# Rows grouped by residue by the host; a fused FFT-convolution and MLP block with unmasked tiles and exchanges through DRAM

## The chip, the cores and the metric

The kernel runs on one core of a Trainium2 chip. The metric is the device time of one execution in microseconds (us), lower is better. Engines are named as in the profile: PE (TensorE matmul), PEld (its weight loads), DVE (VectorE), ACT (ScalarE), POOL (GpSimd), SP (SyncE, which issues all DMAs of this kernel). Data is bfloat16, sums are float32 in PSUM, which has eight banks of 128x512 float32.

## The reference

All activations are 2048 tokens by 512 channels, batch 1.

```python
def _A_ref(q, k, v, shift_k, ssm_k, ssm_D):
    k_shift = 0                              # 4-tap causal shift of k along the tokens
    for t in range(4):
        k_shift = k_shift + k_pad[:, t:t + S, :] * shift_k[:, 3 - t]
    kv = k_shift * v
    # causal convolution of kv with ssm_k along the tokens, by FFT of length 4096
    y = irfft(rfft(pad(kv)) * rfft(pad(ssm_k)))[:, :S, :]
    y = y + kv * ssm_D
    return q * y

def _B_ref(x, w1, w2, w3, w4):               # w1, w2: 512x512, w3: 512x1792, w4: 1792x512
    h = gelu(layernorm(x) @ w1)
    # four groups of 128 channels, moved by -1, +1, -2, +2 tokens
    hs = concat([g0, g1, g2, g3]) @ w2
    x1 = x + hs
    return x1 + gelu(layernorm(x1) @ w3) @ w4

h  = A_q + _A_ref(layernorm(A_q), A_k, A_v, A_shift_k, A_ssm_k, A_ssm_D)
h2 = h + _B_ref(layernorm(h), B_w1, B_w2, B_w3, B_w4)
```

## The kernel before

**Halves and rows.** A token has the number 1024*s + 8*p + b: half s (0 or 1), partition p (0 to 127), block b (0 to 7). The two halves are called first (s=0) and second (s=1). The long convolution is done by halves: A0 and A1 are the transforms of the two halves of kv, F0 and F1 those of the filter. The first half of the output needs A0*F0, the second A0*F1 + A1*F0.

**Tasks.** The body describes some 800 tasks (`add(name, engines, function, dependencies, ...)`) and then emits them in an order written out by hand in the string `ORDER`, where each word gives a task, its engine and its PSUM banks or buffers. Each engine works off its own words strictly in that order. The names used below:

- `S1(sig,b,hp)`, step 1 of a transform (L397): 8 matmuls of 128 rows by 32 columns, N=512, with tables `f1` whose entries are masked so that only rows p of the right residue modulo 4 count. There are 8 tasks for each of F0, A0, F1, A1. `E1` copies their result from PSUM (L266; two banks, 128x1024).
- `X(sig,g,kl)` (L412): a DMA within SBUF, from each fourth partition of `z1` (32 of them) to each second one of `z2` (64), 256 KB. 8 for each signal.
- `S2(sig,kl)` (L420): 16 matmuls of 64 rows by 32 columns. `E2` copies their result (L266); for F1 it is instead a "fold" of two DVE operations (L432) that subtract and add the result of F0.
- `P(s,kl,...)` (L481): products of spectra on DVE, 128x1024, 16 for the first half and 32 for the second. `I2` (L493): 32 matmuls of 32 rows by 32 columns, N=512, 8 tasks for the first half and 16 for the second. `EV` copies (L266).
- `XI(s,kl)` (L503): a DMA within SBUF, 512 KB, four for each half. `I1(s,b)` (L511): the last inverse step, 8 matmuls of 64 rows by 128 columns, masked table `f2`.
- `K` (L449) and `KV` (L457): the shift of k as matmuls with diagonal matrices, and the product with v on DVE. `Q`: statistics of q (L516).
- `H` (L619): the row h on DVE. `HS`, `uw`, `rr`, `hn`: its statistics and normalisation factors over ACT, DVE and POOL. `hb`: the normalised row (L655, L653). `LT` and `TE`: its transpose, either on PE (L671) with a copy, or by two DMAs to DRAM (L664) and a transposing DMA back (L666), as the set `BYDMA` says.
- `W` (L700), `U`: w1 and gelu. `X2` (L729), `S` (L732), `SS`, `R` (L736): w2, the sum, its statistics, the residual. `lb`, `LX`, `EX`: second normalisation and transpose.
- `M` (L781), `G` (L785), `O` (L793), `Z` (L795), `OUT` (L797): w3 for two chunks of 128 features over 256 tokens, gelu, w4 over 14 chunks, the last sum, the store. 56 tasks M, 16 tasks O.
- `Lw1` to `Lw4` and the other loads: L275.

```python
    def step1(b, hp, src):
        def f(e, sl):
            for hh in range(2):
                for t in range(2):
                    for b0 in range(2):
                        j = 2 * t + b0
                        nc.tensor.matmul(ps[32 * j:32 * j + 32, sl[hh], :], lhsT=f1t[:, 4 * t + 2 * hp + hh, :],
                                         rhs=src(2 * b + b0), start=True, stop=True)
```

Of the kernel before, what the change touches and what calls it, by code (L numbers as in the profile page):

```python
# [9 lines left out]
P = 128  # L10
# [6 lines left out]
XW = 258  # L17
KW = NB * 129 + 4
# [13 lines left out]
029P7 004S 030P 031V 067P01 069P23 005S 033A 068A 041V 042G 070A 003S 037V 008S 036V 040V 063P45 002S 064A 065P67 066A 059P01 046V 099P30 043V 000S  # L32
060A 047V 001S 007S 006S 034G 038A 032V 044V 035G 105P2 010S 100V 091P71 061P01 039A 055P45 106V 009S 048A 021S 092V 056A 340V 101P6 102V 103P3 104V
045A 062A 097P2 098V 015S 022S 342V 023S 343V 093P7 057P45 019S 053G 119P01 058A 120A 095P6 049G 050V 121P23 051A 094V 054G 017S 122A 115P45 117P01
118A 024S 078S 096V 111P67 113P23 114A 116V 107P45 112V 109P01 110A 108V 074S 088P6723 090V 089A 345V 077S 071S 073S 075S 085P0145 087V 079P6723 127S
086A 130S 128S 123S 081A 344V 219P10 220V 080A 131P2345 133A 132V 124S 134P6701 135V 136A 072S 076S 082P2345 083A 084A 223P1 125S 144V0 129S 137P6723
020S 227P01 138A 143V1 146V2 147V3 139A 145P45670 148P 231P3 224V 149M 150A 228V 346V 152V0 012S 126S 187P01 189P45 188A 190A 153V1 155V2 018S 232V
014S 195P67 011S 183P01 196V 185P23 184A 186V 013S 191P45 192A 151S 025S 156V3 140P6701 142A 141A 154P23451 157P 347V 225P1 016S 197P67 158M 159A 198A
221P0 201S 161V0 162V1 226V 199S 200S 193P23 194A 341V 163P45670 202S 348G 165V2 164V3 166P 168A 167A 222V 160S 233P1 204S 229P0 170V0 171V1 174V2
239P23 173V3 203S 349G 172P45671 234V 240A 175P 230V 177A 176V 350G 354G0 207P0123 052A 208V 206S 209V 235P67 216P4501 217V 236A 351G1 241P67 242A  # L40
271V0 169S 339G 205S 243P23 244A 178S 179P54 218V 237P67 238A 355V 360G0 247P23 336S 352V 357G1 335S 180P10 361V 358V 356A 338S 245P67 248A 353A 375V
249P45 181P03 246A 366G0 367V 250A 182P12 255S 363G1 251S 364V 376G 377V 362A 359A 372G0 365A 252S 213P4567 215V 378A0 369G1 379P30 381A1 373V 374A
026S 027S 382P2 380A 370V 272V1 259P6701 254S 383A 260A 388G 389G 390G 214V 274V2 275V3 258S 386P3 371A 387A 210P4567 212V 211V 256S 261A 273P01230
391A0 392P71 394A1 395P6 276P 277V0 413G 414G 393A 396A 368A 278V1 262P4567 281V2 415G 401G 253S 402G 403G 280V3 263A 028S 279P 257S 282P 283M 284A
416V0 399P5 400A 384P4 385A 418S 417V1 419S 286V0 268P0123 420S0 264V 269A 397P7 398A 287V1 289V2 270V 404G0 290V3 265P4501 266A 288P23671 291P 406S
423P5 405A1 292V0 424A 293V1 296V2 267A 294P 421P4 295V3 297P 422A 285S 298A 407S 513P5 302V0 301V1 303P01230 304V2 408S0 305V3 306P 299A 509P4 514V
307V0 308V1 411P5 515A 409P7 510V 511A 310V2 311V3 309P 312P 412A 317V0 410A 521P7 313A 300S 314A 517P6 316V1 320V2 319V3 318P01451 522V 321P 322V0
525P3 337S 573G 574G 575G 579A0 576A1 323V1 325V2 577P70 578A 529P2 580P7 315S 326V3 523A 324P 581A 518V 519A 602G 603G 604G 605G0 327P 329A 328A
582P70 588P6 594P5 430V 431V 429V 584P4 426V 585A 330S 583A 425V 592P1 593A 586P0 427V 589A 587A 428V 432V 433V 590P4 591A 526V 530V 434G 527V 606A1
331P76 332P43 333P21 531A 435V 439G0 595A 516V 440V 599P5 436A1 441A 437V 445G0 442G1 630V 438V 446V 451A0 443V 608S 596P0 631G 632G 607S 609S0 600V0  # L50
601S 460G 461G 334P37 444A 447A 473G 452V 448A1 633V0 635S 610P60 614P1 634V1 611A 616P5 620P6 449V 612P4 450V 457G0 453V 454A1 618P2 615A 462G 466A0
613A 617A 458V 622P7 636S 637S1 638P10 644P5 623A 455V 463V1 464P70 465A 621A 459V 619A 524V 640P4 456V 467P3 645A 646P7 474G 475V 477G1 479S 468V
469P6 471P5 497V 520V 498G 624P3 476A0 499V 478S 528V 480S0 472A 470A 500A1 625V0 502S 533P6 534V 485G 501A0 503S 504S1 537P5 538V 648P3 650P6 649A
539A 535V 483P5 484A 486G 487V 642P3 643A 489V0 491S 481P2 647A 488G1 627P5 658G 659G 660G 482A 512V 597V1 532V 662A0 507P7 490S 492S0 641A 661A1 663S
508A 505P4 495P0 493P7 506A 541P4 545P3 626S 546V 639A 494A 496A 553P7 557P2 561P3 651A 549P6 547A 554V 542V 543A 742V 743G 562V 563A 598S 555A 558V
744V 745A1 550V 569P4 565P7 566V 664S 665S0 666P30 667A 674P2 675A 678P6 652P7 655P3 560V 746V0 748S 628V0 672P5 564V 629S 747S 749S1 676P2 570V 571V
750P40 751A 668P1 669A 548V 756P0 551V 757A 686G 687G 688V 677A 690V0 692S 752P4 753A 689V1 552V 673A 670P1 671A 559V 760P2 761A 762P5 691S 714V 715G
716V 754P4 718G0 717V1 693S0 758P2 759A 694P10 696P0 653V0 654S 704P7 719S 568V 679A 705A 680P2 700P7 540V 695A 536V 763A 702P6 698P5 755A 767P4 720S
656V1 567V 657S 699A 701A 770G 771G 697A 706P7 721S1 722P50 772G 773G0 730P3 774G1 731A 556V 776S 724P1 725A 544V 775S 683P0 684V0 777S0 734P3 703A
764P6 707A 778P70 784P1 685S 728P0 785A 735A 765V0 766S 711P6 681V1 782P1 572V 783A 712V0 713S 682S 732P3 733A 726P6 729A 768V0 769S 727A 708P2 709V1  # L60
710S 723A 788P6 789A 739P5 740V0 741S 790P6 786P4 791A 787A 780P5 781A 736P6 737V0 738S 779A 792P7 793V1 794S 795P6 796V0 797S
# [3 lines left out]
class Plan:  # L65
# [4 lines left out]
    def add(self, name, opts, fn, deps=(), take=(), drop=(), size=0, mode=0, port="", mate=None):  # L70
        n = len(self.t)
        t = dict(mate=mate, n=n, name=name, opts=opts, fn=fn, deps=set(), take=list(take), drop=[], size=size, mode=mode, port=port)
        for d in deps:
            t["deps"].add(self.by[d])
        for d, part, *kind in drop:
            m = self.by[d]
            t["deps"].add(m)
            t["drop"].append((m, kind[0] if kind else self.t[m]["take"][0][0], part))
        self.by[name] = n
        self.t.append(t)  # L80
# [20 lines left out]
def body(ctx, tc, fx, kt, q, v, sd, w1, w2, w3, w4, out):  # L101
# [26 lines left out]
    w4s = raw("w4s", FC * D)[:].rearrange("p (f d) -> p f d", f=FC)  # L128
    z_t = ct("z_t", 2, D, dt=F32)
    hnT = ct("hnT", 2, DC, 256)  # L130

    q_sb = r_q[:].rearrange("p (s b d) -> p s b d", s=2, b=NB)
    fxs = view(r_h, 0, G, "p (s b d) -> p s b d", s=2, b=NB)
    v_sb = r_v[:].rearrange("p (s b d) -> p s b d", s=2, b=NB)
    kw = r_k[:].rearrange("p (s c x) -> p s c x", s=2, c=DC)
    kT = [[kw[:, s, c, 0:NB * 129].rearrange("p (b x) -> p b x", b=NB) for c in range(DC)] for s in range(2)]
# [709 lines left out]
```

## Time and profile before

| | |
|---|---|
| three executions, us | 221.14, 223.44, 222.48 (median 222.48) |
| profiled execution, span | 221.2 us, 5913 instructions |
| busy: PE, DVE, ACT, POOL | 200.6, 145.3, 134.9, 67.3 us |
| mean granted TensorE clock | 0.974 |
| DMA, mean over the span | 156 GB/s |

The profiled execution's own time is its span, 221.2 us, near the lowest of the three times. PE is busy for 91% of it, but not evenly: in the stretch from 49.5 to 82.5 us it is busy for 24.8 of 33 us, and the clock granted there falls to 0.69, 0.53 and 0.85 in three pieces of 5.5 us. From 100 us to 217.5 us PE has no idle time. The last matmul ends at 217.5 us; the last sum, store and end follow.

### The profile page before, as it was taken

How to read it: one execution, taken by the hardware profiler on the slowest of the kernel's cores; microseconds unless marked ns; L12 is line 12 of the kernel's file. 1: busy time of each engine (PE TensorE's matmuls, PEld its weight loads, DVE VectorE, ACT ScalarE, POOL GpSimd, SP SyncE). 2: the span in 40 equal slices, each digit the busy share in tenths (PEclk: the TensorE clock that was granted, in tenths of full speed). 3: DMA queues.
4: the chain of work that ended last, by engine and by line, in shares of the span. 5: the costliest groups of instructions: out<-in, count | busy, mean ns of one | idle time of the engine just before them, and what ended most of it. 6: DMA issues, size and time to landing. Idle time of an engine off the chain costs nothing.

```text
span 221.2 us, 5913 instructions
## 1 busy us (share of the span) xinstructions
PE 200.6 (91%) x2372; PEld 118.7 (54%) x2372; DVE 145.3 (66%) x320; ACT 134.9 (61%) x214; POOL 67.3 (30%) x187
## 2 busy tenths in 40 slices
PE   6889578996867799999999999999999999999993
PEld 4454234451223255558548958746588666665641
DVE  7898989999499899899899348059765001312121
ACT  4799889988498979687956646655063323123400
POOL 7342000093276680234685345003125000000000
PEclk9999999999695899999999999999999999999998
DMA  6996798869927535973234154341415402111001
GB/s 193 363 394 271 286 291 318 309 244 307 426 115 268 187 83 160 269 303 98 50 74 95 27 113 102 89 104 46 91 32 142 98 2 45 47 50 47 24 24 47
DMA packets 35996, 34.47 MB, mean 156 GB/s; under 512 B 26753, under 2 KB 28802, under 8 KB 35714
## 3 DMA queue, kind: packets, MB, share of 16 engines
q1 hardware_dynamic: 35970, 34.11, 48.6%
q8 instruction: 18, 0.29, 0.6%
q14 instruction: 8, 0.07, 0.1%
HBM read 13.13 MB, written 5.24 MB: 83 GB/s over the span
## 4 chain that ended last, share of the span: by engine, by line
PE 67%; DMA 11%; SPq 6%; ACT 6%; DVE 5%; issue 2%; POOL 0%; DVEq 0%
PE ps L781 22%; PE ps L793 22%; PE ps L729 6%; PE ps L700 5%; PE ps L493 4%; SPq L412 4%; DMA r_h<-in_fx_dram 3%; SPq L275 3%; DMA r_k<-in_kt_dram 3%; DMA r_x<-r_y 3%; PE ps L511 3%; DVE r_f L432 2%; PE ps L397 2%; ACT r_y L266 2%; DMA r_f<-r_y 2%
## 5 line engine op out<-in xcount | busy, mean ns | idle before, releaser
L781 PE MATMUL ps<-r_dg,r_k 128*128 128x256 bf16 x448 | 51.4, 273 | 0.0
L781 PEld LDWEIGHTS <-r_k 128*128 128x128 bf16 x448 | 43.6, 98 | 7.8 <-issue 0.7
L785 ACT ACTIVATE r_f<-ps 128x512 bf16<-128x512 f32 x26 | 14.9, 598 | 27.8 <-PE ps L781 27.8
L793 PE MATMUL ps<-w4s,r_f 128*128 128x512 bf16 x104 | 24.1, 379 | 0.0
L481 DVE TENSOR_TENSOR r_p<-r_a,r_f 128x1024 bf16<-128x1024 bf16 x32 | 20.8, 694 | 1.0 <-PE ps L493 0.9
L266 ACT CAST r_y<-ps 128x1024 bf16<-128x1024 f32 x19 | 18.6, 1022 | 4.6 <-PE ps L397 4.1
L493 PE MATMUL ps<-r_p,ttab 32*32 32x512 bf16 x768 | 15.8, 379 | 1.4 <-ACT r_x L266 0.6
L700 PE MATMUL ps<-hnT,r_v 128*128 128x256 bf16 x128 | 16.5, 281 | 0.5 <-DMA hnT<-dhb 0.5
L795 DVE TENSOR_TENSOR r_kv<-ps,r_v 128x512 bf16<-128x512 f32 x5 | 3.4, 686 | 20.5 <-PE ps L793 20.5
L795 DVE TENSOR_TENSOR r_kv<-ps,r_a 128x512 bf16<-128x512 f32 x6 | 4.2, 692 | 19.3 <-PE ps L793 17.3
L449 PE MATMUL ps<-r_dg,r_k 128*128 128x256 bf16 (+3 forms) x112 | 15.8, 288 | 1.0 <-ACT r_dg L314 0.5
L785 ACT ACTIVATE r_x<-ps 128x512 bf16<-128x512 f32 x16 | 9.2, 599 | 12.2 <-PE ps L781 12.2
L793 PEld LDWEIGHTS <-r_f 128*128 128x128 bf16 x104 | 10.2, 98 | 11.8
L266 ACT CAST r_vs<-ps 128x1024 bf16<-128x1024 f32 (+1 forms) x12 | 14.3, 1228 | 2.4 <-PE ps L493 1.9
L700 PEld LDWEIGHTS <-r_v 128*128 128x128 bf16 x128 | 12.5, 100 | 5.1 <-issue 2.0
L793 PE MATMUL ps<-w4s,r_x 128*128 128x512 bf16 x64 | 15.1, 379 | 0.0
L729 PE MATMUL ps<-r_v,r_h 128*128 128x512 bf16 x64 | 15.0, 380 | 0.0
L449 PEld LDWEIGHTS <-r_k 128*128 128x128 bf16 x112 | 9.5, 98 | 8.9 <-issue 4.6
L266 ACT CAST r_x<-ps 128x1024 bf16<-128x1024 f32 x14 | 13.7, 1017 | 0.7 <-PE ps L397 0.4
L397 PEld LDWEIGHTS <-f 128*32 128x32 bf16 x256 | 6.2, 99 | 12.6 <-issue 7.3
L493 PEld LDWEIGHTS <-ttab 32*32 32x32 bf16 x768 | 8.3, 88 | 8.7 <-issue 6.0
L793 PE MATMUL ps<-w4s,r_kv 128*128 128x512 bf16 x56 | 12.6, 379 | 0.0
(180 smaller groups left out, 343.8 us busy)
## 6 DMA issues: line engine op xcount, KB each, us to landing
r_k<-in_kt_dram SPq DMA_DIRECT2D x8, 259.0 KB, 5.6
r_h<-in_fx_dram SPq DMA_DIRECT2D x8, 256.0 KB, 4.9
r_v<-in_v_dram SPq DMA_DIRECT2D x4, 512.0 KB, 6.2
r_q<-in_q_dram SPq DMA_DIRECT2D x8, 256.0 KB, 6.4
r_f<-r_x SPq DMA_DIRECT2D x8, 256.0 KB, 3.0
r_a<-r_y SPq DMA_DIRECT2D x8, 256.0 KB, 3.5
r_x<-r_vs SPq DMA_DIRECT2D x4, 512.0 KB, 3.5
r_f<-r_y SPq DMA_DIRECT2D x8, 256.0 KB, 4.0
```

What stands on the lines that cost most here:

```text
L266: (act.copy if e in "AM" else on[e].tensor_copy)(o, i)
L397: nc.tensor.matmul(ps[32 * j:32 * j + 32, sl[hh], :], lhsT=f1t[:, 4 * t + 2 * hp + hh, :], rhs=src(2 * b + b0), start=True, stop=True)
L412: nc.sync.dma_start(z2[sig][g:P:2, kl, :, :], z1[sig][kl:P:4, 2 * g:2 * g + 2, :, :])
L449: nc.tensor.matmul(o[:, (d + j0) * P:(d + j1 + 1) * P], lhsT=kT[s][c][:, bb, x:x + P], rhs=diag[:, c, j0:j1 + 1, :].rearrange("p j x -> p ...
L481: on[e].tensor_tensor(out=prs[:, sl[0], :, :], in0=sp[a][:, kl, t, :, :], in1=gv, op=MUL)
L493: nc.tensor.matmul(ps[c:c + 32, bk[h], :], lhsT=ttab[32 * h:32 * h + 32, 2 * kl + t, 2 if x else xx, 32 * b0:32 * b0 + 32], rhs=prs[32 * h ...
L700: nc.tensor.matmul(ps[:, sl[0], j * 256:(j + 1) * 256], lhsT=w1s[:, k, m * P:(m + 1) * P], rhs=hnT[:, k_, k, :], start=(k == 0), stop=(k = ...
L729: nc.tensor.matmul(ps[:, sl[0], :], lhsT=h1T[:, m, bb, x:x + P], rhs=w2s[:, m, :], start=(m == 0), stop=(m == DC - 1))
L781: nc.tensor.matmul(ps[:, sl[0], j * 256:(j + 1) * 256], lhsT=w3s[:, k, fc * P:(fc + 1) * P], rhs=lnT[:, k_, k, :], start=(k == 0), stop=(k ...
L785: act.activation(gb(gi, 2 * fp, 2), ps[:, got(("M", s, p, fp))[0], :].rearrange("p (j x) -> p j x", j=2), ACT.Gelu_apprx_tanh)
L793: nc.tensor.matmul(ps[:, sl[0], :], lhsT=gb(gi, fc)[:, 0, (b % 2) * P:(b % 2 + 1) * P], rhs=w4s[:, fc, :], start=(fc == 0), stop=(fc == FC ...
L795: add(("Z", s, b), {V: 0.61}, lambda e, sl, b=b: vec.tensor_tensor(out=obt[sl[0]], in0=ps[:, got(("O", s, b))[0], :], in1=h_sb[s][:, b, :] ...
```

## The change

1. The host orders the 128 rows of each half by their residue modulo 4 (`rows`): each residue becomes a run of 32 partitions. The output is put back in order by the host. The tables are built for the new order on the device, with a second one, `ftb`, for F1 and A1 (tasks `wtv`, `wta`, `wt`, `cow`).
2. Step 1 of F1 and A1 (`step1r`) uses unmasked tiles of 32 rows by 32 columns, 16 to a source: four tasks of 16 matmuls for A1, four of 32 for F1. For F1 the second source is F0's input with a turned table `s1g`, and the fold goes away: `E2(F1)` is a copy like the others.
3. The exchange after it (`forward1r`): eight writes `XW` of 256 KB from 128 partitions to a DRAM tile, and four reads `XR` of 512 KB to 128 partitions. A read waits for all eight writes.
4. The exchange before the second half's last inverse step: eight writes `XIW` of 256 KB to DRAM, four reads `XIR` of 512 KB. `I1(1,b)` is then 8 matmuls of 64 rows by 32 columns with an unmasked table `f2u`, and waits for its own `XIR(b)`.
5. SBUF is laid out anew, with more buffers (four for normalised rows, three for transposed ones, six for the gelu results). The rows of the first half's blocks 4 to 7 are transposed on PE and no longer by DMA. The gelu of w1 of the two halves lies in two tiles whose edge columns small POOL and DVE copies exchange (`edge0`, `edge1`, `ed0`, `ed1`, `exa`, `exb`). The w4 load is split in two; `Lw3` has no new dependency but another place in SP's order.
6. `ORDER` is written out anew throughout.

```diff
+    def step1r(u, srcs):
+        t, g = divmod(u, 2)
+        def f(e, sl):
+            for i, (src, tab) in enumerate(srcs):
+                for r in range(4):
+                    for j in range(4):
+                        nc.tensor.matmul(ps[32 * j:32 * j + 32, sl[r], :], lhsT=tab[32 * r:32 * r + 32, 32 * t:32 * t + 32], rhs=src(4 * g + j)[32 * r:32 * r + 32, :],
+                                         start=(i == 0), stop=(i == len(srcs) - 1))
...
+    def forward1r(sig, srcs, sdeps, zdeps, xdeps, sdrop=None):
+        zd = scr.tile([P, 16, D], BF16, name="zd" + sig)
+        zx = zd[:].rearrange("(t r g y) k d -> t g (y k) r d", t=2, r=4, g=2)
+        for u in range(4):
...
+                add(("XW", sig, u, hp), {SP: 0.6}, lambda e, s, u=u, hp=hp: nc.sync.dma_start(zx[u // 2, u % 2, :, 2 * hp:2 * hp + 2, :], z1[sig][:, u, 2 * hp:2 * hp + 2, :]),
+                    [("E1", sig, u, hp)], size=310)
+        for kl in range(4):
+            add(("XR", sig, kl), {SP: 0.6}, lambda e, s, kl=kl: nc.sync.dma_start(z2[sig][:, kl, :, :], zd[:, 4 * kl:4 * kl + 4, :]),
+                [("XW", sig, u, hp) for u in range(4) for hp in range(2)] + list(xdeps), size=620)
...
-                if sig == "F1":
-                    def fold(e, sl, n=n, kl=kl, t=t):
-                        for r, op in ((0, SUB), (1, ADD)):
-                            vec.tensor_tensor(out=sp[sig][:, kl, t, r, :], in0=ps[:, got(n)[2 * t + r], :], in1=sp["F0"][:, kl, t, 1 - r, :], op=op)
...
+            if s:
+                for hp in range(2):
+                    add(("XIW", kl, hp), {SP: 0.6}, lambda e, sl, kl=kl, n=n, hp=hp: nc.sync.dma_start(wx[hp, kl], vst[:, got(n, "vs")[0], 2 * hp:2 * hp + 2, :]),
+                        [("EV", s, kl, hp)], size=310, drop=[(n, 0, "vs")])
...
+            add(("XIR", b), {SP: 0.6}, lambda e, sl, b=b: nc.sync.dma_start(wv[1][:, :, b, :], wd[:].rearrange("p (r b) d -> b p r d", b=4)[b]),
+                [("XIW", kl, hp) for kl in range(4) for hp in range(2)] + [("XW", "A1", x, hp) for x in range(4) for hp in range(2)], size=620)
...
+                    if s:
+                        nc.tensor.matmul(ps[32 * h:32 * h + 32, sl[b0], :], lhsT=f2u[r, :], rhs=wv[1][r, h, b, :], start=True, stop=True)
...
-        add(("I1", 1, b), {PEc: 0.88}, inv1(1, b), ([("I1", 1, b - 1)] if b else []) + [("XI", 1, kl) for kl in range(4)], take=[("ps", 2)], mode=4)
+        add(("I1", 1, b), {PEc: 0.24}, inv1(1, b), ["f2", ("XIR", b)] + ([("I1", 1, b - 1)] if b else [("O", 0, x) for g in (0, 2) for x in MLP[g]]), take=[("ps", 2)], mode=2)
...
-    BYDMA = {("hb", 0, 2), ("hb", 0, 3), ("hb", 1, 1), ("hb", 1, 2), ("hb", 1, 3), ("lb", 0, 1), ("lb", 0, 2), ("lb", 0, 3),
+    BYDMA = {("hb", 1, 1), ("hb", 1, 2), ("hb", 1, 3), ("lb", 0, 1), ("lb", 0, 2), ("lb", 0, 3),
...
+    rows = _np.arange(P).reshape(32, 4).T.reshape(-1)
...
+    return r.results[0]["out_0_dram"][:, _np.argsort(rows)].reshape(1, S, D)
```

Pieces of the new order, with the numbers of `ORDER` replaced by names. PE, from the end of the first half's inverse step on:

```
I1(0,0) S1(A1,0) I1(0,1) S1(A1,1) I1(0,2) S1(A1,2) I1(0,3) S1(A1,3) S2(F1,2) LT LT S2(F1,1) W W LT LT S2(F1,0) LT LT LT W LT W W
S2(A1,0) W I2(1,0,0) S2(A1,1) I2(1,0,1) I2(1,0,2) W I2(1,0,3) X2 I2(1,1,0) I2(1,1,1) W X2 I2(1,1,2) I2(1,1,3) X2 X2 S2(A1,2) X2 X2
S2(F1,3) LX LX S2(A1,3) M(0,0) x5 I2(1,2,0) I2(1,2,1) M(0,0) x2 I2(1,2,2) I2(1,2,3) O O I2(1,3,0) I2(1,3,1) M(0,1) I2(1,3,2) M(0,1) x2
I2(1,3,3) M(0,1) x4 M(0,2) O O I1(1,0) M I1(1,1) M M I1(1,2) I1(1,3) M M LT(1,0) LT(1,1) M W(1,0) x2 O O X2(0,6) X2(0,7) W(1,1) x2 ...
```

SP, second half:

```
... XW(A1,1,1) XR(F1,2) XR(F1,1) XW(A1) x3 XR(F1,0) XW(A1) x2 XR(A1,0) XR(A1,1) Lw2 Lq XR(A1,3) XR(F1,3) XR(A1,2) Lq XIW(0,0) Lw3 Lq
XIW(0,1) XIW(1,0) Lw4 Lw4b XIW(1,1) LX(0,3) Lq LX(0,2) XIW(2,0) EX(0,2) XIW(2,1) LX LX EX(0,4) XIW(3,0) OUT XIW(3,1) XIR(0) ... XIR(3)
```

DVE, the tasks before `H(0,1)`: in the order before 16 KV, 8 Q, 17 P, 10 copies E1/E2/EV, 4 folds and table work; in the new one 16 KV, 8 Q, 16 P, 12 copies, no fold and table work. From `H(0,1)` on, in the order before up to the last P of the second half: 8 H, 31 P, 4 folds, 2 copies, 3 S, 1 uw, 1 hn, 2 hb. In the new order from `H(0,1)` up to `EX(0,0)`, the copy in front of the first M: 8 H, 17 P, 3 copies, 6 S, 4 uw, 3 hn, 4 hb, 1 Y, 2 HS, 1 SS, 1 ux, 1 lb, 5 transposed copies (TE, EX).

## The prediction

> **What bounds the kernel now.** First I read the table of stretches, to see where PE has idle time.
>
> ```profile
> 49.50:55.00 5.50, 3.59 (x88) 1.06 (x59) 5.29 (x9) 4.67 (x7) 2.43 (x7) 1.00 0.96 312
> 55.00:60.50 5.50, 4.31 (x32) 1.29 (x32) 3.02 (x7) 2.41 (x4) 1.45 (x2) 0.69 1.04 424
> 66.00:71.50 5.50, 3.94 (x32) 2.00 (x32) 5.50 (x12) 4.93 (x11) 3.36 (x12) 0.53 0.75 264
> 77.00:82.50 5.50, 4.75 (x92) 2.84 (x87) 5.50 (x10) 4.42 (x6) 4.85 (x12) 1.00 0.29 62
> 100.00:120.00 20.00, 20.00 (x168) 13.00 (x153) 18.59 (x55) 14.05 (x27) 13.92 (x35) 1.00 0.34 86
> 180.00:217.50 37.50, 37.48 (x233) 22.60 (x231) 6.79 (x10) 8.80 (x16) 0.00 (x0) 1.00 0.13 39
> ```
>
> The columns are busy time of PE, PEld, DVE, ACT and POOL, then clock and DMA. Up to some 83 us DVE is the full engine (5.50 of 5.50) and PE is not; from 100 us on PE is full to the end. The chain of waits says the same:
>
> ```profile
> 99.11 1.06 PE ps L493 x64
> 100.18 6.22 PE ps L781 x56
> ...
> 208.42 9.08 PE ps L793 x42
> 217.50 0.02 issue
> 217.52 0.69 DVE r_kv L795
> ```
>
> So the span is: the time at which the first M (L781) can start, 100.1 us, plus the PE work left from there, 117.4 us, plus a tail of 3.7 us (sum, store, end). The change is worth what it takes from the first two. The groups by form give the prices:
>
> ```profile
> L493 PE MATMUL ps<-r_p,ttab 32*32 32x512 bf16 x768 | 15.8, 379 | 1.4 <-ACT r_x L266 0.6 <-DVE r_p L481 0.6
> L397 PE MATMUL ps<-r_kv,f 128*32 128x512 bf16 x128 | 9.1, 407 | 0.8 <-ACT r_y L266 0.6
> L511 PE MATMUL ps<-r_y,f 64*128 64x512 bf16 x32 | 3.8, 377 | 0.0
> L432 DVE TENSOR_TENSOR r_f<-ps,r_f 128x512 bf16<-128x512 f32 x16 | 10.0, 681 | 1.1 <-issue 1.1
> ```
>
> **PE, part by part.** The mean counts the pipeline; what counts is the spacing in a streak. 64 matmuls of L493 take 1.15 us (18 ns each), 56 of L397 3.49 us (62 ns), 8 of L511 0.93 us, 16 of L420 0.6 us. A1's step 1 goes from 64 x 62 ns = 4.0 us to 64 x 18 = 1.2; F1's from 4.0 to 128 x 18 = 2.3. The trace has no 8 matmuls of 64 rows by 32 columns in `I1`'s place, but L420's are that shape: half of 0.6, so 4 x 0.3 = 1.2 against 3.7. The four added transposes of blocks 4 to 7 cost 4 x 0.22 = 0.9 (4 matmuls of L671). Sum: 2.8 + 1.7 + 2.5 - 0.9 = 6.1 us of PE less. Only `I1`'s 2.5 us lies in the full stretch. The bounds for the new tiles are the 18 ns taken and the 62 ns of L397. A rule of the Trainium skill (TensorE: Matmul & The Clock Gate, section "Wait — 56ns, not 53.3ns?") speaks against part of this: matmul starts are never closer than about 25 ns. The row above, with 18 ns for tiles of this very shape, goes against it; by the rule step 1 would save 1.4 us less, outside the full stretch.
>
> **DVE before the first M.** As engine lists are strict, I add the DVE tasks of both orders. Spacing in streaks: P 0.63, KV 0.62, Q 0.61, a copy 1.15, a fold 2 x 0.605, H and S 0.67. Up to `H(0,1)` the old list has 17 P, 10 copies, 4 folds, the new one 16 P, 12 copies, no fold; with the table work (two diagonals and one table step less, the extra table's mask more, -1.8 together) that is 49.6 against 44.6: 5.0 us less. But H also waits for the exchange in front of `I1(0)`:
>
> ```profile
> 49.92 1.23 DVE L266 CAST r_vs<-ps 128x1024 bf16<-128x1024 f32 x1 [0.21 <-ACT r_y L266]
> 51.21 0.56 SPq L503 DMA_DIRECT2D r_x<-r_vs  x1
> 56.19 1.89 PE L511 MATMUL ps<-r_x,f 64*128 64x512 bf16 x8 [1.71 <-DVE r_f L432]
> 58.19 0.75 DVE L619 SCALAR_TENSOR_TENSOR r_v<-ps,qsd,z_t 128x512 bf16<-128x512 f32 x1 [1.59 <-PE ps L511]
> ```
>
> The last `EV(0)` copy ends at 51.1 with 44.2 us of DVE tasks done, 6.9 us behind the list; the new list has 41.1 us up to the same copy, so it ends at 48.0. Add 0.6 to issue `XI(0,3)`, 3.5 to land (its median), 1.0 for `I1(0,0)`, 0.1: H starts at 53.2, against 58.2. (Before, `I1(0,0)` was held further by a fold that freed its bank late, and ran at a lower clock; both go.)
>
> From H to the copy `EX(0,0)` in front of the first M the new list has 8 H 5.4, 17 P 10.7, 3 copies 3.5, 6 S 4.0, 4 uw 4.0, 3 hn 1.8, 5 hb/lb 1.7, 3 statistics 2.6, 5 transposed copies 1.8, Y 0.5, ux 0.7: 36.6 us. uw and hn are chains of tiny operations between POOL and ACT; the rows bound uw by 0.24 and 1.3, hn by 0.36 and 1.3, and I take 1.0 and 0.6, since three of four uw follow ACT statistics, the long form; the ends give -4 and +3 us. The old list had 37.1 us from H to its last P and took 40.8 (58.2 to 99.0): 3.7 lost to waits, which I keep. First M at 53.2 + 36.6 + 3.7 + 0.2 = 93.7. ACT carries 7 of the 8 F1 copies at 0.93 (6.5 us more), but has 5 to 6 us idle of 33 between 49.5 and 82.5 and loses three other copies; POOL gets table work of some 3.5 us (it is idle from 22 to 44 us) and four hb at 0.77; both stay under DVE's list.
>
> **PE left from the first M.** 56 M x 0.873, 16 O x 3.02, 10 X2 and 8 W x 0.87, 2 transposes 0.4, 4 I1 x 0.3 and, new at this place, 8 I2 x 0.56: 119.0 us (the same sum gives 117.0 for before, measured 117.4). Second-half products that came before the first M now lie behind it and are fed by DVE beside M and O.
>
> **The exchanges.** SP issues 8 more DMAs for F1 and A1, 8 more for the last exchange, one more for w4, and six fewer for blocks 4 to 7: 17 x 0.58 - 4 x 0.4 - 2 x 1.2 = 5.9 us more, on a queue that mostly waits. What matters is what stands behind what.
>
> ```profile
> r_x<-r_vs SPq DMA_DIRECT2D x4, 512.0 KB, 3.5
> r_x<-r_y SPq DMA_DIRECT2D x8, 256.0 KB, 3.9
> dlb<-r_k SPq DMA_DIRECT2D x14, 128.0 KB, 2.1
> r_v<-in_v_dram SPq DMA_DIRECT2D x4, 512.0 KB, 6.2
> r_k<-in_w_dram SPq DMA_DIRECT2D x1, 1792.0 KB, 9.2
> ```
>
> (kind, count, KB, us to landing). No row has these writes and reads. A write of 256 KB to DRAM is bounded by 2.1 (128 KB) and 3.9; I take 2.3, nearest the first. A read of 512 KB lies between 3.5 and 6.2 (loads at a full DMA); I take 3.5, as DMA is at 0.3 where the last exchange falls. The Trainium skill (DMA: Bandwidth & Descriptors, section "Anatomy of one DMA") says that a DMA's fixed time is mostly the target's receipt and that HBM is the slowest target. The rows don't show that: writes to DRAM land in 2.1, those within SBUF in 3.9; by the rule, taken as 3.9 for a write, each exchange would be 1.6 us longer.
>
> *A1*: ACT has 7 copies x 0.93 and 5 HS x 0.74 to do after `I1(0,0)` at 53.1, so the copies end at 63.6; issue, write, issue, read make 7.0: 70.6. DVE wants `S2(A1,0)` only some 22 us after H, 75. Hidden; at the upper prices (11.3) just so.
> *Last exchange*: from `I2(1,3,3)` on: copy 1.3, XIW 0.6, OUT 0.4, XIW 0.6, write 2.3, XIR 0.6, read 3.5 = 9.3. Cover on PE: 5 M and 2 O = 10.4. Hidden by 1.1; the other three reads (1.5 MB, 4 to 6 us) have 3.5 us of cover and cost about 0.5.
> *w3 and w4* are issued behind `XIW(0,0)` and `XIW(1,0)`. From the I2 that ends the first, 0.9 + 0.6 + 0.6 + 9.2 = 11.3 us to w3's landing; DVE needs about 12 to the first M. Taken as 0.5.
> *Second half's transposes* (W(1,2) behind a DMA): 0.5. Together 1.5, bounds 0 and 8.
>
> **Sum.** 93.7 + 119.0 + 1.5 + 3.7 = 217.9 against 221.2: 3.3 us less. The profiled run is 1.3 us under the median, so 222.5 - 3.3 = 219.2 us.
>
> **Rivals.**
> *The exchange takes the place of the wait (slower).* If write and read land at 3.9 and 6.2, the last exchange takes 13.6 against 10.4 of cover: 3.2 us of idle PE in front of `I1(1,0)`, about 2.5 more for the reads behind it at the same rate, and w3, fetched beside them, 1.5 later: 7.2 in place of 1.0. That gives 225.4. It decides once PE idles more than some 4 us there. For it: every cover is nearly equal to its latency. Against: DMA's share is low there.
> *DVE eats the gain (no change).* The list from H has 15 hand-overs with POOL, ACT and PE (4 uw, 3 hn, 4 hb, 4 TE) where the old one had 4; if 7 us are lost in place of 3.7, the result is 222.5. For it: DVE has 36.6 us to do beside 22 us of PE.
> *The PE saving shows in full.* If idle time stays as it is, 6.1 off 222.5: 216.4. For it: more buffers, and DVE waits of 1.5 to 3 us before H could shrink further.
> *The tiles don't pack.* At 62 ns a start, `I1(1)` costs 2.7 more in the full stretch: 221.9. Against: L493.
>
> **How the numbers follow.** Forecast 219.2 (own range 216.5 to 221.5): 0.42. Exchange 0.23, DVE 0.15, full saving 0.15, no packing 0.05. A measurement of this kernel tells about 1% from no change. Faster by over 1% (under 220.3): 0.36 of the forecast and all of the full saving, 0.51. Slower by over 1% (over 224.7): the exchange and some of DVE's, 0.28. Within: 0.21. The range reaches from 214.0 (full saving, with 2 us of waits less) to 226.0.
>
> **What would show it.** Right: step 1 of A1 at about 0.3 us for 16 matmuls, the first M near 94 us with a full DVE before it, PE without idle time from there but for 1 to 3 us around L511's second group, last matmul near 214. Wrong: the first M after 97; more than 4 us idle before the second half's `I1`; an M or O that waits for w3 or w4; PE clock under 1.0 after 95 us.

## The result, and the profile after

The changed kernel takes 231.13 us (median of 4 runs, 229.54 to 232.22) against 222.41 us before (4 runs): a ratio of 1.039, 95% interval 1.031 to 1.048. It is slower by some 9 us; the forecast was 219.2 us, faster by 1.5%. The profiled execution has a span of 228.5 us (221.2 before) and took 230.28 us. Each ratio in this document is to executions of the kernel before that were made beside the runs in question, so medians of different experiments can't be compared with each other.

The table of stretches of the changed kernel, at the times that were shown of before (columns: busy time of PE, PEld, DVE, ACT and POOL, then clock, DMA share, GB/s):

```profile
49.50:55.00 5.50, 4.03 (x141) 2.14 (x109) 4.30 (x5) 3.84 (x5) 0.00 (x0) 1.00 0.83 265
55.00:60.50 5.50, 3.46 (x32) 1.02 (x32) 2.49 (x6) 3.12 (x5) 0.91 (x2) 0.72 0.96 323
66.00:71.50 5.50, 2.02 (x24) 0.92 (x24) 5.00 (x22) 4.79 (x10) 4.02 (x8) 0.65 0.97 328
71.50:77.00 5.50, 5.15 (x37) 3.18 (x38) 2.82 (x15) 4.34 (x8) 2.10 (x3) 0.50 0.44 163
77.00:82.50 5.50, 5.27 (x78) 3.81 (x76) 4.21 (x8) 4.10 (x8) 0.82 (x2) 0.92 0.91 303
100.00:120.00 20.00, 19.82 (x347) 12.46 (x347) 16.88 (x30) 11.74 (x23) 11.21 (x16) 1.00 0.56 158
150.00:180.00 30.00, 27.92 (x221) 21.45 (x221) 19.83 (x58) 16.76 (x37) 8.41 (x20) 1.00 0.50 109
180.00:217.50 37.50, 37.34 (x239) 23.50 (x240) 6.63 (x10) 10.73 (x21) 0.00 (x0) 1.00 0.11 32
```

DVE, which was nearly full between 66 and 82.5 us (busy for 15.38 of 16.50 us), is not so any more: 12.03 of 16.50 us. PE has 2.1 us of idle time between 150 and 180, where it had none. The chain of waits (start, duration, engine, target, line) says what took their places. In it `r_z<-r_vs` is `XI(0,3)`, L564 is `I1` of the first half, L760 `W`, L781 `X2`, L833 `M`; `dhb` and `dlb` are the DRAM tiles of the normalised rows, and `xtx` and `r_dg` the buffers into which DMA transposes them:

```profile
51.88 5.03 DMA r_z<-r_vs
57.04 1.58 PE ps L564 x8
...
73.17 3.57 PE ps L760 x16
...
100.70 4.47 PE ps L833 x40
...
148.41 3.82 DMA xtx<-dhb
152.27 2.79 PE ps L760 x24
156.80 1.56 PE ps L781 x8
158.36 2.94 DMA r_dg<-dlb
161.34 1.03 PE ps L833 x8
170.07 1.68 DVE r_v L788 x2
171.91 3.87 DMA dlb<-nbx
175.86 3.00 DMA r_dg<-dlb
178.90 15.89 PE ps L833 x144
```

Before, the chain was PE alone from 99.11 us on. Now transposes made by DMA stand in it at 148 to 179 us, and ahead of the first `M` (L833, at 100.64) the transfer `XI(0,3)` of 5.03 us. The groups by form show that the tiles themselves are cheap (busy time, mean ns):

```profile
L427 PE MATMUL ps<-r_kv,s 32*32 32x512 bf16 x64 | 2.5, 438 | 0.3 <-DVE r_v L679 0.3
L427 PE MATMUL ps<-r_q,s 32*32 32x512 bf16 x64 | 2.1, 383 | 1.5 <-ACT r_a L265 1.0 <-ACT r_vs L265 0.5
L562 PE MATMUL ps<-r_z,f2u 64*32 64x512 bf16 x32 | 1.6, 387 | 0.0
```

A1's step 1 (r_kv) has 2.5 us busy where 64 of the masked form had 4.5 (half of L397's 9.1), and the last inverse step 1.6 against 3.8. From start to next start, 16 matmuls of F1's step 1 take 0.21 to 0.23 us and 16 of A1's 0.38 us at full clock, 8 of the last step 0.34; the forecast had 0.3 for each. And yet PE's busy time in the whole span is 200.3 us, as before (200.6).

Three marks divide the span, and the experiments below are read by them: P, the first product of the first half on DVE; H, the first `H`; M, the first `M`. "M to last" ends with the last matmul (all in us, from the profiled executions):

| kernel | P | H | M | M to last | span | ratio to before, 95% |
|---|---|---|---|---|---|---|
| before | 30.95 | 58.19 | 100.11 | 117.4 | 221.2 | |
| forecast | | 53.2 | 93.7 | 120.5 | 217.9 | |
| after | 36.17 | 58.73 | 100.64 | 124.4 | 228.5 | 1.039 (1.031 to 1.048) |
| e1 no exchange of F1, A1 | 37.40 | 58.03 | 98.63 | 124.6 | 227.0 | 1.039 (1.029 to 1.048) |
| e2 no last exchange | 38.05 | 60.06 | 101.65 | 124.7 | 230.1 | 1.049 (1.042 to 1.056) |
| e3 late loads | 33.44 | 56.95 | 97.63 | 125.0 | 226.1 | 1.036 (1.028 to 1.044) |
| e4 step 1 twice | 36.43 | 58.68 | 101.54 | 124.0 | 229.0 | 1.045 (1.035 to 1.055) |
| e5 order | 34.00 | 57.29 | 98.47 | 124.0 | 226.0 | 1.031 (1.020 to 1.042) |
| e6 no DMA transposes | 36.96 | 59.65 | 101.48 | 121.5 | 226.6 | 1.030 (1.022 to 1.037) |
| e7 last step x3 | 37.88 | 60.13 | 101.53 | 124.1 | 229.1 | 1.038 (1.029 to 1.047) |
| e8 no late I2 | 36.72 | 58.97 | 100.97 | 122.9 | 227.7 | 1.032 (1.020 to 1.044) |
| e12 short E1(F1) | 36.83 | 59.22 | 101.12 | 123.7 | 228.3 | 1.048 (1.043 to 1.053) |
| e13 short E2(F1) | 36.93 | 59.57 | 99.20 | 124.5 | 227.2 | 1.037 (1.030 to 1.044) |
| e14 three causes out | 34.11 | 57.91 | 98.62 | 121.4 | 223.9 | 1.011 (1.002 to 1.021) |
| before + e9 I1 tiles | 30.17 | 55.94 | 97.34 | 116.6 | 217.6 | 0.999 (0.995 to 1.004) |
| before + e10 folds to ACT | 30.19 | 59.30 | 104.20 | 117.4 | 225.3 | 1.028 (1.023 to 1.034) |
| before + e11 all tiles | 29.71 | 60.93 | 109.15 | 117.9 | 230.7 | 1.047 (1.039 to 1.055) |
| before + e15 no folds | 30.22 | 58.21 | 99.83 | 117.4 | 220.9 | 1.002 (0.997 to 1.007) |

One profiled execution is one draw. In the nine kernels of the changed family whose work up to P is the same (after, e1, e2, e4, e6, e7, e8, e12, e13), P lies anywhere from 36.2 to 38.1. A mark has to move by more than that, or the ratio must, before an edit is credited. The stretches between the marks vary less: where nothing in them was edited, P to H is 22.0 to 22.7 in these kernels, H to M 41.4 to 42.0 (40.7 in e3), M to last 123.7 to 125.0.

### The profile page after: what moved, and what is told of

Same layout as the page of the kernel before. It is cut to its first block, busy times and chain, and to the rows that moved or that the text cites. A ratio compares the mean times of both kernels' runs of the same rounds, so it can differ in the third digit from the quotient of the medians.

```text
span 228.5 us, 6091 instructions
## 1 busy us (share of the span) xinstructions
PE 200.3 (88%) x2437; PEld 117.0 (51%) x2452; DVE 147.8 (65%) x348; ACT 131.9 (58%) x215; POOL 74.8 (33%) x194
## 4 chain that ended last, share of the span: by engine, by line
PE 57%; DVE 14%; ACT 12%; DMA 10%; issue 4%; SPq 1%; POOL 1%; DVEq 0%; POOLq 0%; ACTq 0%
PE ps L846 21%; PE ps L833 13%; PE ps L760 6%; PE ps L536 3%; PE ps L781 3%; DVE r_p L524 3%; ACT r_vs L265 3%; PE ps L417 3%; DMA r_dg<-dlb 3%; ACT r_a L265 2%; PE ps L490 2%; DMA r_z<-r_vs 2%; DVE r_kv L498 2%; ACT r_f L265 2%; PE ps L468 2%
## 5 line engine op out<-in xcount | busy, mean ns | idle before, releaser
L833 PEld LDWEIGHTS <-r_k 128*128 128x128 bf16 x448 | 43.0, 98 | 10.1 <-issue 3.1
L848 DVE TENSOR_TENSOR r_v<-ps,r_v 128x512 bf16<-128x512 f32 x16 | 10.8, 688 | 40.9 <-issue 26.1
L833 PE MATMUL ps<-r_dg,r_k 128*128 128x256 bf16 x280 | 33.2, 273 | 1.1 <-DMA r_dg<-dlb 1.1
L265 ACT CAST r_a<-ps 128x1024 bf16<-128x1024 f32 (+1 forms) x23 | 23.4, 1061 | 3.8 <-PE ps L427 1.7
L265 ACT CAST r_f<-ps 128x1024 bf16<-128x1024 f32 x19 | 18.7, 1018 | 5.5 <-PE ps L468 4.3
L833 PE MATMUL ps<-xtx,r_k 128*128 128x256 bf16 x168 | 20.5, 273 | 0.4 <-DVE qst L568 0.2
L760 PEld LDWEIGHTS <-r_fx 128*128 128x128 bf16 x128 | 12.9, 104 | 5.9 <-issue 2.2
L679 DVE SCALAR_TENSOR_TENSOR r_v<-ps,qsd,z_t 128x512 bf16<-128x512 f32 x16 | 11.5, 748 | 6.5 <-PE ps L564 3.0
L784 DVE SCALAR_TENSOR_TENSOR r_q<-r_v,hrr,ps 128x512 bf16<-128x512 bf16 x16 | 11.6, 741 | 5.5 <-PE ps L781 5.4
L760 PE MATMUL ps<-r_dg,r_fx 128*128 128x256 bf16 x96 | 13.5, 297 | 0.3 <-ACT r_dg L265 0.2
L846 PE MATMUL ps<-w4s,r_v 128*128 128x512 bf16 x54 | 12.2, 379 | 0.1
```

The lines of the kernel that those rows point to most:

```text
L265: (act.copy if e in "AM" else on[e].tensor_copy)(o, i)
L679: vec.scalar_tensor_tensor(out=h_sb[s][:, b, :], in0=ps[:, got(("I1", s, b // 2))[b % 2], :], scalar=qsd[:, i:i + 1], in1=z_t[:, got(("Y", ...
L760: nc.tensor.matmul(ps[:, sl[0], j * 256:(j + 1) * 256], lhsT=w1s[:, k, m * P:(m + 1) * P], rhs=xt[:, k, :], start=(k == 0), stop=(k == DC ...
L784: vec.scalar_tensor_tensor(out=q_sb[:, s, b, :], in0=h_sb[s][:, b, :], scalar=hrr[:, 4 * s + b // 2, 0, b % 2:b % 2 + 1], in1=ps[:, got((" ...
L833: nc.tensor.matmul(ps[:, sl[0], j * 256:(j + 1) * 256], lhsT=w3s[:, k, fc * P:(fc + 1) * P], rhs=xt[:, k, :], start=(k == 0), stop=(k == D ...
L846: nc.tensor.matmul(ps[:, sl[0], :], lhsT=gb[:, fc, (b % 2) * P:(b % 2 + 1) * P], rhs=w4s[:, fc, :], start=(fc == 0), stop=(fc == FC - 1))
```

## The experiments

### The saved work, put into the kernel before

These four are the answer to the forecast's central sum, so they come first. All keep the old order and the old exchange.

**e15, DVE's folds left out:**

```diff
-  for r, op in ((0, SUB), (1, ADD)):
-      vec.tensor_tensor(out=sp[sig][:, kl, t, r, :], in0=ps[:, got(n)[2 * t + r], :], in1=sp["F0"][:, kl, t, 1 - r, :], op=op)
+  vec.tensor_copy(sp[sig][:, kl, t, :, 0:64], pair(got(n), t)[:, :, 0:64])
```

> The kernel before with the folds of E2(F1) left out and nothing on ACT in their place (a copy of 64 columns by DVE stays, some 0.2 us, so that DVE's list is 8 us shorter). It tells apart why e10 got slower. If DVE's saving is worth something by itself and ACT's 7.4 us ate it, the first M comes at 93 to 97 and the time is 214 to 218; if the wait goes to other engines whatever ACT does, the first M stays within 1.5 us of 100.

M came at 99.83 against 100.11, and the ratio is 1.002 (0.997 to 1.007): 8 us less for DVE, and nothing gained. The stretches of before and of e15, in this order, show where the 8 us went:

```profile
50.00:60.00 10.00, 7.08 (x84) 2.22 (x86) 8.02 (x14) 6.17 (x7) 2.97 (x7) 0.83 1.00 364
60.00:80.00 20.00, 15.07 (x272) 7.03 (x268) 17.84 (x40) 18.01 (x33) 13.92 (x35) 0.83 0.53 185
```

```profile
50.00:60.00 10.00, 6.56 (x84) 2.00 (x86) 4.08 (x10) 6.07 (x7) 2.87 (x7) 0.83 0.99 352
60.00:80.00 20.00, 15.29 (x280) 7.10 (x284) 14.58 (x36) 18.46 (x34) 14.82 (x35) 0.83 0.56 193
```

DVE's busy time (third of the five) falls by 3.9 and 3.3 us; the other engines' times move by at most 0.9. From 50 to 60 the folds had lain in the time in which H waits for `XI(0,3)` anyway. The wait that was short while DVE was folding is now long, first before, then two lines of e15:

```profile
DVE r_v L619 <- PE ps L511: 2.8, 2, 1.6
...
DVE r_v L618 <- PE ps L510: 6.1, 2, 4.9
DVE r_f L431 <- issue: 3.2, 1, 3.2
```

(columns of the waits: who waits for whom; us in total, times, longest. L619 of before is L618 of e15.) From H to M it took 41.6 us, as before (41.9), with 3.3 us less of DVE work between 60 and 80 us.

**e10, the folds' place taken by copies on ACT** (`copy(A, sp[sig][:, kl, t, :, :], pair(got(n), t))`):

> The kernel before with the 16 folds of E2(F1) on DVE (10.0 us) replaced by 8 copies on ACT (7.4 us) at the same places of the order (the fold's sum is left out). The forecast counted DVE's list up to the first M as what sets it. If it does, the first M comes 3 to 6 us earlier (94 to 97) and the time is 216 to 219. If ACT, PE and transfers set it as much as DVE, by under 2 us.

The first M came 4.1 us later, not earlier, and the ratio is 1.028. Neither expectation allowed for that. ACT is busy 19.50 of 20 us between 60 and 80. DVE waits for ACT's copies, and above all for I2 on PE (L492), which itself waits 3.2 us for a copy on ACT (0.6 in before):

```profile
DVE r_p L480 <- PE ps L492: 9.8, 4, 8.2
DVE r_v L618 <- PE ps L510: 6.1, 2, 5.6
DVE r_p L480 <- ACT r_f L266: 2.3, 1, 2.3
```

Together e15 and e10 say: in the old order, taking the folds off DVE is worth nothing that the runs can tell, and putting their copies on ACT at these places costs 2.6% (1.028 against 1.002).

**e9, the last inverse step in small tiles:**

```diff
-  nc.tensor.matmul(ps[:, sl[b0], :], lhsT=f2[64 * b0:64 * b0 + 64, h].rearrange("p n q -> p (n q)"), ...
+  nc.tensor.matmul(ps[32 * h:32 * h + 32, sl[b0], :], lhsT=f2[64 * b0:64 * b0 + 64, h, 0:8].rearrange("p n q -> p (n q)"), ...
```

> The kernel before, in its own order, with the second half's I1 made of tiles of 64 rows by 32 columns (8 per block as in the changed kernel, the same numbers of instructions; the rows are not regrouped, so other values come out). The forecast put 2.5 us of saving into the full stretch of PE. If that stretch is full in the order before, the span falls by 2.0 to 2.6 us (ratio about 0.99). If the saving is given back at a wait, as in e7 on the changed kernel, by under 0.8.

The profiled span, 217.6, looks like a gain of 3.6 us, but its M is early already (97.34), ahead of anything that was edited; the timed runs give 0.999 (0.995 to 1.004). M to last fell by 0.8, not by 2.5. PE's busy time from M on fell by 2.9, to 114.48 (a few matmul records are missing), but it now has 2.1 us of idle time there, 1.2 of them just behind M, waiting for `G` on ACT. So the saving is real and is given back.

**e11, all tiles in the order before** (e9, e10 and step 1 of F1 and A1 in tiles of 32 by 32):

> The kernel before, its order and its exchange kept, with all three: I1(1) of e9, no folds as in e10, and step 1 of F1 and A1 in tiles of 32 rows by 32 columns (as many as in the changed kernel; values other ones). It holds what the tiles remove and none of what the order and the exchange through DRAM add. If the tiles' saving can be cashed, 213 to 218 and the whole loss of the changed kernel (9 us and this gain) lies in its order and transfers. If it can't, 220 to 222.

1.047: slower still than e10, though PE has less to do. The guess that the loss "lies in order and transfers" fell: the savings weren't cashed in the old order either, which with all three is as slow as the changed kernel. But e11 holds the copies on ACT, and these alone make 2.8% (e10), so it doesn't price the tiles by themselves; what the rest adds was not isolated. Step 1 in small tiles was not run alone in the old order.

### The changed kernel: ahead of the first M

**e3, three loads later**: `Lk(1,1)`, `Lk(1,3)` and `Lf(1,2)` moved behind X(A0) on SP, and `K(3,1)` behind the first I2 (words 016S, 018S, 013S and 234P of the order).

> The changed kernel with three second-half loads (Lk(1,1), Lk(1,3), Lf(1,2), 0.84 MB) put behind the transfers of X(A0) on SP, and one K behind the first I2. Theory C (the early transfers X(F0), X(A0) are late because 0.84 MB of second-half loads stand between them in a full DMA, 2 us at 400 GB/s): P(0,0) starts at 33.5 to 34.5 in place of 36.2, H(0,1) at 56 to 57 in place of 58.7, first M as much earlier, time 228.5 to 229.5. If the start of the products is set by PE's or ACT's order instead, P(0,0) stays within 0.7 us and the time within 1 us of 231.1.

As theory C had it: P at 33.44, outside the 36.2 to 38.1 of its unchanged relatives, M 3.0 us earlier, span 2.4 less. The ratio, 1.036, can't be told from the 1.039 of after by its interval. The issues on SP's queue and the first product, after and then e3:

```profile
25.56 1.22 SPq L443 DMA_DIRECT2D r_a<-r_a  x2
26.83 0.61 SPq L443 DMA_DIRECT2D r_f<-r_f  x1
27.48 3.85 SPq L443 DMA_DIRECT2D r_a<-r_a  x5
...
36.17 1.29 DVE L524 TENSOR_TENSOR r_p<-r_a,r_f 128x1024 bf16<-128x1024 bf16 x2
```

```profile
23.74 1.18 SPq L443 DMA_DIRECT2D r_a<-r_a  x2
24.97 0.60 SPq L443 DMA_DIRECT2D r_f<-r_f  x1
25.61 3.99 SPq L443 DMA_DIRECT2D r_a<-r_a  x5
...
33.44 2.52 DVE L524 TENSOR_TENSOR r_p<-r_a,r_f 128x1024 bf16<-128x1024 bf16 x4
```

**e5, two more moves**: e3's, then X(F0,1,·) together on SP, and `W(0,0)` behind `LT(0,2)` and `LT(0,4)`.

> The changed kernel with three moves in the written order and all of its tiles kept: the late loads of e3; X(F0,1,0), X(F0,1,2), X(F0,1,3) directly behind X(F0,1,1) on SP; and W(0,0) behind LT(0,2) and LT(0,4) on PE. Theory (the time lost ahead of the first M is DVE waiting for transfers and PE tasks that the order puts too late): P(0,0) at 31.5 to 33 (36.2 after, 33.4 in e3), the wait of DVE for a transpose at 75 to 77 us shrinks from 2.2 (1.7 in e3) to under 1, first M at 95 to 96.5, time 226 to 228. If DVE's list itself or the exchange sets the first M, it stays within 0.7 us of e3's 97.6 and the time at 228 to 229.5.

No gain over e3: P 34.00, M 98.47. The wait for the transpose at 75 us did go, but another of the same size took its place (DVE waiting 2.6 us for ACT, behind the `U` that moved with `W`).

**e1, no exchange of F1 and A1** (step 2 reads `z1`, the DMAs are left out):

> The changed kernel without the exchange of F1 and A1: S2 reads the tiles where step 1's copies left them, the 16 writes to DRAM and 8 reads are left out, so the numbers that come out are other ones. Theory A (the exchange through DRAM is slower than its cover): S2(F1) and S2(A1) come when the copies are done, the 41.9 us from H(0,1) at 58.7 to the first M at 100.6 shrink to 37 to 39, the PE clock stays at 1.0 between 66 and 82 us, time 226 to 228. Theory B (the loss lies ahead of H and in hand-overs of the list): the stretch from H to M stays within 1 us of 41.9 and the time within 1 us of 231.1.

Between the two: M 2.0 us earlier, P to H 20.6 in place of 22.6 (outside the 22.0 to 22.7 of the others), H to M 40.6 in place of 41.9 (hardly below the 40.7 of e3), the clock between 66 and 77 us still at 0.5 to 0.6. The ratio shows no gain. So the exchange is not fully hidden, but it is not the bulk of the loss.

**e4, step 1 twice**:

> The changed kernel with every matmul of F1's and A1's step 1 done twice into the same bank (192 more of 18 ns, 3.5 us of PE; A1 then costs what the masked form cost; values doubled). If step 1 lies off the path, as PE idles beside DVE there, the time stays within 0.7 us of 231.1: the tiles' saving in step 1 was worth nothing. If PE's chain S1, copy, exchange, S2 sets the first M, it rises by 2 to 3.5.

M at 101.5 lies among the kernels without it, and the ratio, 1.045 (1.035 to 1.055), can't be told from the 1.039 of after. H to M, 42.9, is the longest of these kernels, so that about 1 of the 3.5 us added may show. Step 1's saving of 4.5 us was for the most part off the path.

**e12 and e13, shorter copies on ACT**, ahead of H (five copies of E1(F1)) and behind it (seven of E2(F1)):

> The changed kernel with the five copies of F1's step 1 that ACT does made half as long (one bank of two, the other left as it was; some 0.4 us less each, 2 us in all, ahead of H). The forecast said that ACT stays under DVE's list. If ACT, at 5.2 to 5.4 of 5.5 us between 33 and 44, sets the way from the products to H, the stretch from P(0,0) to H shrinks from 22.6 to 20.5 to 21.5; if DVE or XI(0,3)'s transfer sets it, by under 0.6.

> The changed kernel with the seven copies of E2(F1) that ACT does made half as long (half of the columns; some 0.4 us less each, 2.9 us in all, between H and the first M). In e10 the same copies on ACT made DVE wait 8 us for them. If ACT sets the way from H to the first M here too, that stretch shrinks from 41.9 by 1.5 to 3 us; if DVE's list and its hand-overs with PE do, by under 0.7.

e12: P to H 22.4, as it was; shorter copies on ACT gain nothing there. e13: H to M 39.6, the shortest of all, against 40.7 to 42.0; there they do gain, 1.1 to 2.4 of the 2.9 us. The ratio, 1.037, doesn't show it.

### The changed kernel: from the first M on

**e2, no last exchange:**

> The changed kernel without the last exchange (8 writes, 4 reads left out; the last inverse step reads what lies there). By the forecast's cover (10.4 against 9.3 us) and the trace after, which shows no wait in front of the second I1, the exchange itself is hidden: 230 to 231.1. The rival of the forecast (the exchange takes the place of the wait) would give 224 to 226 here. Between them: if its 4 MB only slow w3 and w4 and the transposes through DRAM, 229 to 230.

1.049, no faster. The forecast's main rival, the exchange in place of the wait, is ruled out, and so is the middle case.

**e7, the last step's matmuls three times:**

> The changed kernel with each matmul of the second half's I1 done three times into its bank (64 more of some 37 ns: 2.4 us, about what the masked form cost more). If the last inverse step lies in the full stretch of PE, the span grows by 2.0 to 2.8 us; then the saving of the tiles there was real, and was lost elsewhere. If PE waits there anyway, by under 1.

24 matmuls took 0.82 us to the next start in place of 0.34 for 8, so 1.9 us were added, and M to last stayed at 124.1. The added work went into time in which PE would have waited later. After, and then e7, the waits of PE from 101 us on:

```profile
PE ps L833 <- DMA r_dg<-dlb: 1.1, 2, 0.8
PE ps L760 <- DMA xtx<-dhb: 0.9, 1, 0.9
PE ps L731 <- DVE nbx L715: 0.4, 1, 0.4
PE ps L833 <- DVE qst L568: 0.2, 1, 0.2
```

```profile
PE ps L761 <- DMA xtx<-dhb: 1.4, 1, 1.4
PE ps L468 <- ACT r_f L265: 0.6, 1, 0.6
```

(The 0.6 lies ahead of M.) The wait for `r_dg<-dlb` is gone: PE came later to where it had to wait. From M on its idle time fell from 3.2 to 1.9 us.

**e8, no matmuls in the eight late I2:**

> The changed kernel without the matmuls of the eight I2 tasks behind the first M (kl 2 and 3 of the second half; the copies stay). By the spacing in a streak they are 8 x 0.56 = 4.5 us. If that is their price, the stretch from the first M to the end shrinks by 4.2 to 4.8 us; if each change between the small tiles and the full ones costs PE extra, as the sum of prices that is 5.2 short suggests, by 5.2 to 6.5.

Both were wrong: M to last fell by 1.4 only. PE waits 3.6 us for `r_dg<-dlb` (1.1 before the edit), and it is idle for 2.5 of the 10 us from 110 on, which it had been filling with I2. PE's busy time from M on did fall by 4.9 (121.15 to 116.26), 0.4 more than the 4.5 of the sum of prices; this is all that the run shows of a price of going to and fro between small tiles and full ones.

**e6, no transposes by DMA:**

> The changed kernel with the transposes that DMA makes from DRAM left out (the blocks in BYDMA; the matmuls read what lies in the buffers). From the first M to the end the trace after shows 0.93, 0.22 and 0.83 us of PE waiting for such a transpose, and the sum of the PE prices is 5.2 us short there. If those waits are a loss of their own, that stretch shrinks by 1.8 to 2.2 us; if something else (G, Z, the next S) ends just behind them, by less than 0.8.

M to last 121.5, against 123.7 to 125.0 in the kernels that have them and all of their matmuls: 2.9 us less than after, more than the 2.0 of the waits. PE's idle time there fell from 3.2 to 1.05 us and its busy time from 121.15 to 120.45. It is the largest single loss behind M that was found.

### All three at once

**e14: e3, e1 and e6 together.**

> The changed kernel with the three suspects taken out together: the late loads of e3, no exchange of F1 and A1 as in e1, no transposes by DMA as in e6. Alone they gave 3.0 at the first M (e3), 2.0 from P to H and 1.3 from H to M (e1), 2.9 behind M (e6). If they are separate losses, the span falls from 228.5 by 7 to 9 us, to 219.5 to 221.5, that is to the 221.2 before; if they cover each other, by 3 to 5.

Span 223.9, 4.6 us less; ratio 1.011 (1.002 to 1.021), which doesn't meet the 1.031 to 1.048 of after. Taken out, the three give back 2.8 of the 3.9% by the timed runs, but they cover each other ahead of M: it came at 98.62, later than with e3 alone. And with all three out, it is still no faster than before, although PE and DVE have less to do. The kernel before has an exchange of F1 and A1 and DMA transposes too and pays for them, so the 2.8% are what leaving this work out is worth, not what the change added; the cause of the whole loss stays open to that extent. No experiment points to a version that beats the kernel before.

## Why the prediction was wrong

**DVE before the first M** is the step that failed. It made a clock of a list: 5.0 us fewer tasks up to H, and 36.6 us of tasks from there, put M at 93.7. The measured M is 100.64: 5.5 us too late at H and 1.4 more from H to M. DVE did do 6.0 us less before 100 us (79.3 busy after 5 us, 85.3 before), and waited so much longer. e15 shows that this was in the old kernel already: it gave up 8 us of DVE work for nothing, and from H to M it took 41.6 us in place of 41.9. The chain of waits of before, further up than the prediction shows it, had the warning:

```profile
46.67 3.73 DMA r_f<-r_y
...
51.73 3.07 DVE r_f L432 x5
...
64.72 2.59 DMA r_x<-r_y
...
70.40 2.99 DMA r_x<-r_y
```

Between 36 and 99 us it is a mixture of all engines and DMA, in which the steps on DVE (L432, L481, L619) make 8.3 us. The 5.50 of 5.50 was real, but a part of it was folds filling waits. Of the forecast's own marks, "the first M after 97" came true; the others (PE idle in front of the second I1, an M or O waiting for w3 or w4, a clock under 1.0 after 95) did not.

**ACT "under DVE's list"** failed with it. It was argued from 5 to 6 us of idle time; in e10 the moved copies stand in front of what DVE and PE wait for (M 4.1 us later), and in e13 shorter ones bring M nearer to H.

**H at 53.2** failed term by term. The last `EV(0)` copy ended at 51.9, not 48.0. The forecast kept the 6.9 us by which the old copy lay behind its list, but the products started at 36.17 in place of 30.95, in part because `X(A0)` came behind second-half loads on SP. That is not the whole of it: e3 took the loads away and moved P by 2.7 us, but the copy, with the issue of `XI(0,3)` right behind it, only by 0.5. After and then e3:

```profile
51.88 0.54 SPq L550 DMA_DIRECT2D r_z<-r_vs  x1
...
51.35 0.54 SPq L550 DMA_DIRECT2D r_z<-r_vs  x1
```

What holds the copy then was not isolated. From the start of its issue `XI(0,3)` took 5.0 us in the chain, not 0.6 + 3.5 (4.8 in e15, which has the old exchange, 4.3 in e3; 3.6 in e1 and 3.9 in e14, where nothing of F1 stands beside it). `I1(0,0)` took 1.58 us, not 1.0, in a stretch with a clock of 0.72. And that a fold had held it in before was no time to be gained: in e15, without the folds, it starts at 56.21, released by `XI(0,3)`, against 56.19.

**PE's 6.1 us** were nearly right as a price (step 1 and the last step, by the spacing given above) and wrong as a saving. Step 1 lay off the path, as the forecast said (e4); but so did the 2.5 us of the last step, which it put "in the full stretch" (e7, e9). Full meant that the order had work at hand whenever a chain was late. The total of PE's busy time doesn't show the 6.1 us either: the granted clock between 5 and 100 us was 0.91 against 0.95 before, and the work from the first M on took more than its prices. No run isolates the share of the clock.

**PE left from the first M**: 119.0 of work and 1.5 of stalls were forecast, 124.4 measured. PE is busy for 121.15 of them and idle for 3.2, so the work was priced 2.1 too low and the stalls 1.7. The transposes by DMA, put at 0.5, are worth 2.9 (e6). What makes the work dearer was not isolated; the eight I2 took 4.9 with them in e8, against 4.5 in the sum.

**The exchanges** were mis-sized, but they did not decide. In the DMA groups of after (count, KB, us to landing):

```profile
zdF<-r_a SPq DMA_DIRECT2D x8, 256.0 KB, 3.6
zdA<-r_z SPq DMA_DIRECT2D x8, 256.0 KB, 6.9
r_f<-zdF SPq DMA_DIRECT2D x4, 512.0 KB, 7.7
r_a<-zdA SPq DMA_DIRECT2D x4, 512.0 KB, 5.2
wd<-r_vs SPq DMA_DIRECT2D x8, 256.0 KB, 2.9
r_z<-wd SPq DMA_DIRECT2D x4, 512.0 KB, 5.3
```

The writes were taken at 2.3 and the reads at 3.5. Two of the six lie above the upper bounds of 3.9 and 6.2: A1's writes (6.9) and F1's reads (7.7); the writes and three of the four reads are issued between 61 and 70 us, with a DMA share of 0.89 from 61 to 72. The last exchange, at 2.9 and 5.3, still cost nothing that shows (e2). The Trainium skill's rule weighed there (DMA: Bandwidth & Descriptors, section "Anatomy of one DMA": the fixed time is mostly the target's receipt, and HBM is the slowest target; the section is about DMAs issued by GpSimd, here SP issues all) can't be told by these rows from DMA being busy: the same kind of write took 2.9 and 6.9.

**The rivals**: the exchange in place of the wait was wrong in its place (e2), though its sign was right. "DVE eats the gain" was nearest: from H to M 5.3 us were lost to waits (41.9 less 36.6), where the forecast kept 3.7 and this rival took 7. But the larger part of the delay lies ahead of H, and its 222.5 is far from 231.1. The rule set against the forecast (the Trainium skill, TensorE: Matmul & The Clock Gate, section "Wait — 56ns, not 53.3ns?": however short the moving side, no starts closer than about 25 ns) does not hold for these tiles: 16 of step 1's went by in 0.23 us in several places (16 matmuls from 53.73, the next group from 53.96), that is 14 ns a start. "The tiles don't pack" had a slip in its price: 32 matmuls at 62 ns make 2.0 us, 0.8 more than the 1.2 of the sum and not 2.7. Two more slips decide nothing: DVE's list from H adds up to 36.7, and A1's copies end at 63.3.

## What to carry to other kernels

A busy engine in a stretch is not the same as an engine on the path: look at the whole chain of waits before adding up its list, and test on the kernel as it is, by leaving the work out, what its absence is worth before building its replacement (e15 would have said so in one run). In this kernel, with PE, DVE, ACT and DMA all busy for 50 to 100% of the stretch in question, saved work turned into a wait (e15), while copies moved to ACT cost 2.6% (e10 against e15). And a new order has to be priced queue by queue: the loads ahead of a transfer, and the transposes that have lost their cover.

## What the runs showed of the hardware

- In the changed kernel PE had nothing to do from 66 to 69 us. The granted clock was 0.91 from 66 to 68 us and 0.50 from 68 to 77, and 16 matmuls of `W` took 3.57 us where the same 16 take 1.91 from 80.39 on. That the gap lowered the clock is not shown: in e1, without the exchange and with no gap of more than 1.3 us there, the clock was 0.50 from 66 to 71.5 and 0.61 in the next stretch, although PE was busy for 3.63 of 5.5 us just before.
- Writes of the same size to DRAM landed at very different times. In the last exchange the first four (issued from 89.5 to 101.2 us; DMA share 0.87 from 85 to 105) took 4.3 us (median), the last two (DMA share 0.43 from 118 to 126) 2.5. A1's eight, issued within 9 us (DMA share 0.89 from 61 to 72), took 6.9.
- The early part, with a DMA share of 0.78 to 1.04 from 10 to 30 us, varies by 1.9 us between executions of the same instructions (P at 36.2 to 38.1), more than most edits moved it.
